# Row sums and AV of a batch in one PSUM tile, batch 0 loaded in two row ranges, and a new opening order, in attention followed by an ELU feed-forward

## The chip, the cores and the metric

The kernel runs on one core of one Trainium2 chip. The metric is the device time of the run in microseconds (us): the median of seven runs of the kernel before is 354.44 us, the lowest 353.19, the highest 355.32. A core has engines that run side by side, each through its own list of instructions in order: PE (TensorE, matrix products, which also loads weights, PEld in the profile), ACT (ScalarE), DVE (VectorE), POOL (GpSimd) and SP (SyncE). They wait for each other through semaphores. PE writes into PSUM only, which ACT and DVE read. DMA transfers are issued from POOL, SP or ACT and move on their own.

## The reference

There are 8 batches of 8 heads with 576 queries, 64 elements a head, and 16 extra keys and values ("beacons") that stand ahead of the 576 ordinary ones and that every query may see. The attention output, 4608 tokens of 512, goes through a feed-forward network with 2048 hidden elements.

```python
k_all = np.concatenate([beacon_k, k], axis=2)
v_all = np.concatenate([beacon_v, v], axis=2)
scores = scale * np.matmul(q, k_all.transpose(0, 1, 3, 2))
scores = np.where(causal, -1000000000.0, scores)
scores = scores - scores.max(-1, keepdims=True)
a = np.exp(scores)
a /= a.sum(-1, keepdims=True) + 1e-09
attn_out = np.matmul(a, v_all)
x = attn_out.transpose(0, 2, 1, 3).reshape(B * S, H * D)
h = x @ w_in
g = np.where(h > 0.0, h, np.exp(np.minimum(h, 0.0)) - 1.0)
return g @ w_out
```

## The kernel before

The kernel is written as small named steps, and two strings give the order in which they are issued. A word such as `S.1.0.2` calls step `S` with the arguments 1, 0, 2. Every engine takes its part of each step in that order. So a step that waits on one engine holds all that stands behind it on that engine.

The first string is the opening: it loads, computes attention of batches 0 to 2 and starts batch 3, and runs the feed-forward of the first 1024 tokens. The second, `BODY`, is repeated for b = 3 to 9. In it `b` is the batch and the token tile at hand, `z` is b - 1, `c` is b + 1 and `d` is b + 2. Bodies 3 to 7 hold attention and feed-forward, 8 and 9 what is left of the feed-forward. Steps whose batch or tile doesn't exist are skipped.

The steps, with their lines:

- `lk`, `load_qk` (line 119): loads q and k of a batch. Batches 0 to 2 go to staging tiles, six rows to a partition, in two or more groups of heads. Later batches are copied to a scratch tensor in DRAM (line 583) and read back by transposing DMAs from SP (`lt`, line 591), for which POOL also writes the padding and the beacon keys. There are two buffers for each kind of staging tile, and the qkd tiles of `lt` use the same ones.
- `T` (line 227): PE turns staged q and k of two heads (a pair), so that the 64 elements of a head lie across partitions. `ck` (ACT) and `cq` (DVE) copy the turned halves from PSUM to an SBUF tile, `cb` (DVE) adds the beacon keys. For batch 0, pairs 0 to 2, ACT takes k and DVE takes q; otherwise ACT copies both in one instruction.
- `S` (line 268): scores of a pair, keys across partitions, queries along the row. The causal part of the score matrix has 1664 columns for the five chunks of keys, cut into four groups of 416. `x` (line 288, ACT) is the exponential of a group for both heads, `m` (DVE) zeroes what lies above the diagonal.
- `quad` (line 307): for four heads at once, 32 output rows each, the products over all chunks of keys, with ones (row sums, step `L`) or with one half of v (steps `W`). Each chunk is one group of four matmuls that stand side by side in the array. `L` and `W` cover queries 0 to 511 only; the last 64 queries of a batch are taken by `R` (line 414) for both groups of heads, row sums and both halves at once. A tile of tag `S` has two PSUM banks: `L` and the first `W` share one, the second `W` shares one with `R`.
- `n` (ACT, lines 349 and 352): reciprocal of the row sums by a logarithm and an exponential. `M` (DVE, line 386, and line 406 for R): output times reciprocal, into the tile of feed-forward input. Batch 0 is cut at query 256 into the parts `A` and `B`, because the first two token tiles have 256 tokens.
- `F` (line 438): one PSUM bank of hidden elements. `e` and either `u` (ACT) with `k` (DVE, line 463), or `r` and `g` (both DVE), form the ELU.
- `G` (line 484): output product of the first two token tiles. `o` copies it to SBUF and `s` stores it from SP. Later tiles use `Q` (line 548), a block scheme with seven products in place of eight for the 2 x 2 blocks, with sums of weights (`wt`) and of inputs (`Z`, line 505), and `J` for its results.
- `load_v`, `load_wi`, `load_wo` (lines 126, 142, 149): loads of v and of the two weights from POOL. `warm` issues products of zeros on PE.

All loads with a conversion of type, and the scratch copies, are issued from POOL in the order in which they are written. Besides the tag `S` (two tiles of two banks), PSUM has two banks of tag `hps` and two of tag `ops`.

Of the kernel before, what the change touches and what calls it, by code (L numbers as in the profile page):

```python
# [8 lines left out]
FP32 = mybir.dt.float32  # L9
# [8 lines left out]
def kernel(  # L18
# [12 lines left out]
    P = 128  # L31
# [20 lines left out]
    Q1 = 512  # L52
    QR = S - Q1
# [71 lines left out]

    def load_v(b, js):
        if js[0] == 0:
            st.setdefault(b, [None] * 3)[2] = stage.tile([P, NKC, H, D], FP16, tag="v16", name="v16")
            nc.gpsimd.dma_start(  # L129
                out=st[b][2][0:NB, 0, :, :], in_=beacon_v[b].rearrange("h n d -> n h d"))  # L130
        for j in js:
# [3 lines left out]
                out=st[b][2][r0:r0 + n, j, :, :],  # L135
# [28 lines left out]
    for t in qks:  # L164
        nc.vector.memset(t[:, 1, SK:P * NKC], 0.0)
# [537 lines left out]
```

## Time and profile before

| What | Value |
|---|---|
| Median of seven runs | 354.44 us |
| The profiled execution, its own time | 354.55 us |
| Span of the profiled execution | 352.8 us |
| Granted TensorE clock, mean | 0.998 |
| Instructions in the trace | 10230 |
| Moved by DMA | 34.75 MB, mean 98 GB/s |
| F, 128x512 columns (L438) | 512 matmuls, 131.5 us busy |
| Row sums and AV (L316) | 1680 matmuls of batches 1 to 7 in the code, ten groups of four to a quad with R, and 192 of batch 0 |
| Exponentials of scores (L289) | 128, 106.4 us busy, mean 905 ns |
| Copies of turned q and k on ACT (L254, L258) | 3 and 9, 2.0 and 10.5 us busy |

The span runs from the first to the last instruction, and what lies around it, 1.75 us here, is in the run's time. "Busy" is the union of an engine's instructions. Instructions of one engine can overlap in the records, so the distance from one start to the next is often shorter than the duration printed. In rows of the timeline the columns are the start and the length of a stretch in us, the engine, line and operation, what is written and read with its shape, the number of instructions, and in brackets the idle time ahead of it and who ended it. In rows of the chain they are start, length, and what the time went to. "issue" is time in which the engine waited for nothing that the profile shows.

### The profile page before, as it was taken

Reading aid. Unit: us, or ns where it says so; the run is one execution under the profiler, and the core shown is the slowest. Engines: PE = TensorE matmul, PEld = TensorE weight load, DVE = VectorE, ACT = ScalarE, POOL = GpSimd, SP = SyncE. Lnnn points to the kernel's source line nnn. Section 1 sums busy time; section 2 is a strip of 40 time slices with the busy share of each in tenths; the row PEclk is TensorE's granted clock in tenths of the full one; section 3 lists DMA queues with packets and bytes.
Section 4 is the critical chain, followed back from the end, with each engine's and each line's share of the span. In section 5 each row is a group of like instructions: output and inputs, shape, how many; then the busy total and the mean of one; then the engine's idle time right before and its main releaser. Section 6 shows DMA issues by size and latency. Waiting matters only on the chain.

```text
span 352.8 us, 10230 instructions
## 1 busy us (share of the span) xinstructions
PE 339.3 (96%) x4331; PEld 210.2 (60%) x4331; DVE 232.7 (66%) x523; ACT 291.9 (83%) x495; POOL 86.8 (25%) x120
## 2 busy tenths in 40 slices
PE   8989999899999999999999989999999999999995
PEld 3557665544456566556665556556665666666684
DVE  2446874557887767766777566757676767667661
ACT  1999999699989997999799969997999587686731
POOL 8868355460074007300540022000000000000000
PEclk9999999999999999999999999999999999999999
DMA  8999999999399309990799429601100010010022
GB/s 119 165 193 180 182 205 158 144 179 169 68 159 130 46 32 90 172 168 8 95 169 157 38 65 140 123 2 33 61 32 2 32 59 32 31 61 30 33 89 91
DMA packets 127278, 34.75 MB, mean 98 GB/s; under 512 B 110848, under 2 KB 125696, under 8 KB 127232
## 3 DMA queue, kind: packets, MB, share of 16 engines
q0 software_dynamic: 93120, 18.49, 62.8%
q1 hardware_dynamic: 33536, 15.47, 20.8%
q8 instruction: 34, 0.56, 0.6%
q10 hardware_dynamic: 576, 0.13, 0.2%
q14 instruction: 12, 0.10, 0.1%
HBM read 37.22 MB, written 15.34 MB: 149 GB/s over the span
## 4 chain that ended last, share of the span: by engine, by line
PE 66%; ACT 18%; DVE 5%; POOL 4%; DMA 3%; issue 3%; DVEq 0%; POOLq 0%
PE hps L438 28%; PE ops L548 23%; ACT et L289 9%; PE lt L316 5%; PE sc L279 4%; ACT r L453 4%; ACT e L448 4%; PE ut L316 4%; DMA kst<-in_k_dram 2%; DVE gt L463 2%; DVE xT L386 2%; PE ops L484 1%; POOL v L134 1%; DMA w_in<-in_moe_w_in_dram 1%; ACT qk L258 1%
## 5 line engine op out<-in xcount | busy, mean ns | idle before, releaser
L438 PE MATMUL hps<-xT,w_in 128*128 128x512 f16 (+1 forms) x640 | 147.7, 359 | 0.1
L463 DVE SCALAR_TENSOR_TENSOR gt<-e,r 128x512 f16<-128x512 f32 x132 | 91.2, 691 | 58.3 <-ACT r L453 57.5
L289 ACT ACTIVATE et<-sc 128x832 f16<-128x832 f32 x128 | 106.4, 905 | 2.6 <-PE sc L279 2.6
L448 ACT ACTIVATE e<-hps 128x512 f32<-128x512 f32 x144 | 88.9, 618 | 21.5 <-PE hps L438 20.3
L548 PEld LDWEIGHTS <-gt 128*128 128x128 f16 x768 | 75.1, 98 | 28.9
L438 PEld LDWEIGHTS <-w_in 128*128 128x128 f16 x640 | 56.3, 98 | 46.1 <-issue 6.7
L453 ACT ACTIVATE r<-hps 128x512 f16<-128x512 f32 x132 | 82.1, 622 | 0.0
L305 DVE TENSOR_TENSOR et<-et,triu 128x256 f16<-128x256 f16 (+2 forms) x164 | 40.7, 272 | 20.8 <-ACT et L289 18.0
L548 PE MATMUL ops<-wt,gt 128*128 128x256 f16 x384 | 52.5, 273 | 0.0
L548 PE MATMUL ops<-w_out,gt 128*128 128x256 f16 x384 | 51.4, 273 | 0.0
L134 POOL DMA_DIRECT2D v<-in_v_dram x40 | 33.7, 858 | 3.3 <-DMA kst<-in_k_dram 2.6
L505 DVE TENSOR_TENSOR gt<-gt 128x1024 f16<-128x1024 f16 x48 | 32.6, 684 | 0.0
L316 PEld LDWEIGHTS <-v 128*32 128x32 f16 x1248 | 21.2, 94 | 10.5 <-issue 5.2
L279 PE MATMUL sc<-qkd 64*128 64x208 bf16 (+5 forms) x320 | 22.6, 253 | 2.3 <-DVE xT L386 1.8
L129 POOL DMA_DIRECT2D v<-in_beacon_v_dram x8 | 4.3, 542 | 67.1 <-PE ut L316 58.8
L316 PE MATMUL ut<-et,v 128*32 128x64 f16 (+6 forms) x840 | 17.1, 225 | 3.0 <-issue 2.6
L279 PEld LDWEIGHTS <-qkd 64*128 64x128 bf16 x320 | 11.3, 94 | 14.2 <-issue 10.0
L557 ACT COPY sm<-ops 128x512 f32<-128x512 f32 x24 | 15.3, 637 | 5.0 <-PE ops L548 5.0
L564 DVE TENSOR_TENSOR osb<-ops,sm 128x512 f32<-128x512 f32 x24 | 16.4, 684 | 4.3 <-issue 3.3
L386 DVE TENSOR_TENSOR xT<-lt,rl 128x448 f16<-128x448 f32 (+6 forms) x28 | 10.6, 418 | 11.2 <-ACT rl L352 11.2
L548 PE MATMUL ops<-w_out,s 128*128 128x256 f16 x128 | 17.6, 273 | 0.0
L279 PE MATMUL sc<-qk 64*128 64x208 bf16 (+11 forms) x208 | 15.4, 245 | 2.0 <-ACT et L289 1.5
(63 smaller groups left out, 280.0 us busy)
## 6 DMA issues: line engine op xcount, KB each, us to landing
out_dram<-osb SPq DMA_DIRECT2D x36, 256.0 KB, 2.2
v<-in_v_dram POOLq DMA_DIRECT2D x24, 128.0 KB, 5.1
scr<-in_q_dram POOLq DMA_DIRECT2D x5, 576.0 KB, 12.7
scr<-in_k_dram POOLq DMA_DIRECT2D x5, 576.0 KB, 15.5
w_in<-in_moe_w_in_dram POOLq DMA_DIRECT2D x16, 128.0 KB, 5.3
w_out<-in_moe_w_out_dram POOLq DMA_DIRECT2D x4, 512.0 KB, 10.9
v<-in_v_dram POOLq DMA_DIRECT2D x8, 112.0 KB, 4.4
v<-in_v_dram POOLq DMA_DIRECT2D x8, 80.0 KB, 6.3
```

Of the source, the lines that this page charges most:

```text
L134: nc.gpsimd.dma_start(out=st[b][2][r0:r0 + n, j, :, :], in_=v[b, :, ilo[j]:ilo[j] + n, :].rearrange("h s d -> s h d"),)
L279: nc.tensor.matmul(out=s[:, h, a - c0:e - c0], lhsT=t[D * h:D * (h + 1), 1, P * j:P * (j + 1)], rhs=t[D * h:D * (h + 1), 0, NB + qa + a - ...
L289: nc.scalar.activation(out=ets[b, p][:, :, GW * g:GW * (g + 1)], in_=sc[b, p, g][:, :, 0:GW], func=AFT.Exp, bias=0.0, scale=SCALE)
L305: nc.vector.tensor_tensor(out=o, in0=o, in1=triu[0:kc[j], :, t0:t0 + e - a], op=ALU.mult)
L316: nc.tensor.matmul(out=t[32 * i:32 * (i + 1), a - qa:e - qa], lhsT=ones[0:kc[j], :] if half is None else v16[0:kc[j], j, h, 32 * half:32 * ...
L386: nc.vector.tensor_tensor(out=x_tile(k)[:, cc, tok - TT * k:to - TT * k], in0=u[:, o:o + to - tok], in1=r[:, o:o + to - tok], op=ALU.mult)
L438: nc.tensor.matmul(out=h[:, n_, :], lhsT=w_in16[:, cc, P * fc:P * (fc + 1)], rhs=xt[k][:, cc, a - TT * k:e - TT * k], start=(cc == 0), sto ...
L448: nc.scalar.activation(out=eb[t, i], in_=flat(hp[t, i]), func=AFT.Exp, bias=0.0, scale=1.0)
L453: nc.scalar.activation(out=rb[t, i], in_=flat(hp[t, i]), func=AFT.Relu, bias=0.0, scale=1.0)
L463: nc.vector.scalar_tensor_tensor(out=half(t, i), in0=eb[t, i], scalar=1.0, in1=rb[t, i], op0=ALU.subtract, op1=ALU.min)
L505: nc.vector.tensor_tensor(out=o_, in0=a_, in1=b_, op=op_)
L548: nc.tensor.matmul(out=xy[t, n_][:, qd, :], lhsT=lw[:, P * qd:P * (qd + 1)], rhs=wt_[:, c, :], start=(first and qd == 0 and c == 0), stop= ...
```

## The change

It has three parts.

1. `R` is gone. A quad now covers all 576 queries in one tile of two banks: queries 0 to 111 end at the bank's border, queries 112 to 575 lie in the second bank. `L` and each `W` have such a tile of their own, so six tiles of tag `S` a batch in place of four. `n` works on 576 columns, `M` on all queries of its half. In part `B` of batch 0, both groups of heads share a tile.
2. q and k of batch 0 are loaded and turned in two ranges of rows: 0 to 255 with two rows to a partition (128 partitions), 256 to 575 with four rows (80 partitions). `T`, `ck` and `cq` take the range as an argument and copy q and k together. `w_in` is loaded in chunks of 512 hidden columns (16 DMAs as before), and loads are steps of the order.
3. The opening string is new. Most turned tiles are copied by `cq` on DVE: of the batches 1 and 2 all but one, of batch 0 six halves of eight. `lk.3.0` and the end of v of batches 2 and 3 stand late on POOL, behind the first rows of v of batch 3. In the body `W.b.0.1` and the last two `W` have moved behind the steps `S.b.3` and `S.c.0`.

```diff
+    SEGS = {0: [(0, CUT, 2), (CUT, S, 4)]}
+
+    def segs(b):
+        return SEGS.get(b, [(0, S, R)])
+
+    def seg_view(t, b, n_):
+        a, e, r = segs(b)[n_]
+        m = (e - a) // r
+        return t[0:m, OFF[b, n_]:OFF[b, n_] + H * r * D].rearrange("p (h r d) -> p h r d", h=H, r=r)
...
+    def load_qk(b, n_, h0, h1):
+        if b not in st:
+            st[b] = [stage.tile([P, H * R * D], BF16, tag=tag, name=tag) for tag in ("qst", "kst")]
+        a, e, r = segs(b)[n_]
         for src, dst in ((q, st[b][0]), (k, st[b][1])):
             nc.gpsimd.dma_start(
-                out=dst[:, h0:h1, :, :].rearrange("p h r d -> p h (r d)"),
-                in_=src[b, h0:h1, :, :].rearrange("h (p r) d -> p h (r d)", r=R),
+                out=seg_view(dst, b, n_)[:, h0:h1, :, :].rearrange("p h r d -> p h (r d)"),
+                in_=src[b, h0:h1, a:e, :].rearrange("h (p r) d -> p h (r d)", r=r),
             )
...
-    def load_wi(fa, fe):
-
+    def load_wi(c):
+        f_ = slice(512 * c, 512 * (c + 1))
         for g in range(2):
-            for i in range(4):
-                nc.gpsimd.dma_start(
-                    out=w_in16[32 * i:32 * (i + 1), 2 * g:2 * g + 2, fa:fe], in_=wi_v[i, :, g, :, fa:fe])
+            for t in range(2):
+                nc.gpsimd.dma_start(out=w_in16[:, 2 * g + t, f_], in_=wi_v[:, :, g, t, f_])
 
     def load_wo(i):
...
-    @step
-    def T(b, p):
-        if b == 0 and p < 3:
-            tps[b, p] = bank("hps", BF16, "tq"), bank("hps", BF16, "tk")
-            dsts = tps[b, p]
...
+    @step
+    def T(b, p, n_):
+        a, e, r_ = segs(b)[n_]
+        m_ = (e - a) // r_
+        if b == 0:
+            t_ = bank("hps", BF16, "tq")[:, 0:2 * (e - a)].rearrange("c (i s) -> c i s", i=2)
         else:
-            tps[b, p] = psum.tile([P, 2, 1024], BF16, tag="S", name="tp")
-            dsts = tps[b, p][:, 0, :], tps[b, p][:, 1, :]
-        for dst, src in zip(dsts, st[b]):
-            for r in range(R):
+            t_ = psum.tile([P, 2, 1024], BF16, tag="S", name="tp")[:, :, 0:e - a]
+        tps[b, p, n_] = t_
+        for i, src in enumerate(st[b]):
+            sv = seg_view(src, b, n_)
+            for r in range(r_):
                 for h in range(2):
                     nc.tensor.transpose(
-                        out=dst[D * h:D * (h + 1), PR * r:PR * (r + 1)],
-                        in_=src[:, 2 * p + h, r, :],
-                        identity=identb[0:PR, 0:PR],
+                        out=t_[D * h:D * (h + 1), i, m_ * r:m_ * (r + 1)],
+                        in_=sv[:, 2 * p + h, r, :],
+                        identity=identb[0:m_, 0:m_],
                     )
 
     @step
...
+    def drain(f, b, p, n_):
+        a, e, r = segs(b)[n_]
+        f(out=qkT[b, p][:, :, NB + a:NB + e].rearrange("c i (p r) -> c i p r", r=r),
+          in_=tps[b, p, n_].rearrange("c i (r p) -> c i p r", r=r))
+
+    @step
+    def ck(b, p, n_):
+        drain(nc.scalar.copy, b, p, n_)
+
+    @step
+    def cq(b, p, n_):
+        drain(nc.vector.tensor_copy, b, p, n_)
...
+    QA = ilo[1]
+
+    def quads(b, g, half, name):
+
+        t = psum.tile([P, 1024], FP32, tag="S", name=name)[:, 512 - QA:512 - QA + S]
+        quad(b, g, 0, QA, t[:, 0:QA], half, True)
+        quad(b, g, QA, S, t[:, QA:S], half, True)
+        return t
...
         else:
-            t = psum.tile([P, 2, 512], FP32, tag="S", name="lt")
-            quad(b, g, 0, Q1, t[:, 0, :], None, True)
-            lt[b, g], ut[b, g, 0] = t[:, 0, :], t[:, 1, :]
+            lt[b, g] = quads(b, g, None, "lt")
...
         elif g == "B":
-            g = i[0]
-            t = ut[b, "B", g, half] = bank("ops", name="ub")
-            quad(b, g, CUT, S, t[:, 0:S - CUT], half, True)
+            t = psum.tile([P, 2, 512], FP32, tag="S", name="ub")
+            for i in range(2):
+                quad(b, i, CUT, S, t[:, i, 0:S - CUT], half, True)
+            ut[b, g, half] = t[:, :, 0:S - CUT]
         else:
-            if half:
-                t = psum.tile([P, 2, 512], FP32, tag="S", name="ut")
-                ut[b, g, 1], ut[b, "R"] = t[:, 0, :], t[:, 1, :]
-            quad(b, g, 0, Q1, ut[b, g, half], half, True)
+            ut[b, g, half] = quads(b, g, half, "ut")
...
         elif g == "B":
-            g, half = i
-            scale_out(b, 2 * g + half, CUT, S, ut[b, "B", g, half][:, 0:S - CUT],
-                      rls[b, "B"][:, (S - CUT) * g:(S - CUT) * (g + 1)])
-        elif g == "R":
-            tok = b * S + Q1
-            k = tok // TT
-            for half in range(2):
+            half = i[0]
+            r_ = rls[b, g][:, 0:2 * (S - CUT)].rearrange("c (g q) -> c g q", g=2)
+            for k, a_, e_ in ((0, CUT, TT), (1, TT, S)):
                 nc.vector.tensor_tensor(
-                    out=x_tile(k)[:, half::2, tok - TT * k:tok - TT * k + QR],
-                    in0=ut[b, "R"][:, 2 * QR * (half + 1):2 * QR * (half + 2)].rearrange("c (g q) -> c g q", g=2),
-                    in1=rls[b, "R"][:, 0:2 * QR].rearrange("c (g q) -> c g q", g=2), op=ALU.mult)
+                    out=x_tile(k)[:, half::2, a_ - TT * k:e_ - TT * k], in0=ut[b, g, half][:, :, a_ - CUT:e_ - CUT],
+                    in1=r_[:, :, a_ - CUT:e_ - CUT], op=ALU.mult)
         else:
-            scale_out(b, 2 * g + i[0], 0, Q1, ut[b, g, i[0]], rls[b, g][:, 0:Q1])
-
-    @step
-    def R_(b):
-
-        t = ut[b, "R"]
-        for n, half in enumerate((None, 0, 1)):
-            for g in range(2):
-                c = QR * (2 * n + g)
-                quad(b, g, Q1, S, t[:, c:c + QR], half, c == 0)
-        lt[b, "R"] = t[:, 0:2 * QR]
-    op["R"] = R_
+            scale_out(b, 2 * g + i[0], 0, S, ut[b, g, i[0]], rls[b, g][:, 0:S])
...
     run("""
-    warm.12 bt bk cb.0.0 cb.0.1 cb.0.3 cb.0.2 warm.3 T.0.0 ck.0.0 cq.0.0 warm.4.64 S.0.0.0
-    S.0.0.1 T.0.1 x.0.0.0 cq.0.1 m.0.0.0 x.0.0.1 S.0.0.2 warm.1.64 S.0.0.3 ck.0.1 x.0.0.2 cb.1.0
-    warm.1.64 T.0.2 S.0.1.0 x.0.0.3 x.0.1.0 warm.1.64 S.0.1.1 m.0.0.2 cq.0.2 x.0.1.1 warm.2.64
...
+    lq.0.0.0.4 warm.12 ident bt bk cb.0.0 lq.0.1.0.4 warm.8 cb.0.1 cb.0.2 T.0.1.0 T.0.0.0
+    cq.0.0.0 warm.2 ck.0.1.0 S.0.1.0 x.0.1.0 cb.1.1 S.0.0.0 T.0.1.1 cq.0.1.1 T.0.0.1 warm.2
+    x.0.0.0 S.0.1.2 lq.0.0.4.8 T.0.3.0 cq.0.0.1 tri m.0.0.0 lv.0.2 S.0.1.1 T.0.2.0 x.0.1.2
+    S.0.0.2 x.0.1.1 cq.0.2.0 x.0.0.2 S.0.1.3 x.0.1.3 cb.0.3 cq.0.3.0 m.0.1.2 warm.1 lq.0.1.4.8
+    warm.1 S.0.3.0 lq.1.0.0.4 x.0.3.0 S.0.0.1 x.0.0.1 T.0.3.1 cq.0.3.1 S.0.2.0 warm.2 warm.1
+    m.0.1.3 S.0.3.2 x.0.2.0 m.0.2.0 warm.2 S.0.0.3 cb.1.0 m.0.3.0 T.0.2.1 m.0.1.0 S.0.3.3
+    T.1.0.0 cq.1.0.0 T.1.1.0 cq.1.1.0 x.0.3.2 x.0.0.3 m.0.0.3 L.0.A x.0.3.3 lv.0.0.1 W.0.A.0
+    wi.0 ck.0.2.1 m.0.3.2 S.0.2.2 n.0.A M.0.A.0 W.0.A.1 M.0.A.1 m.0.0.2 S.1.1.0 lv.0.3.4 x.0.2.2
+    S.0.3.1 S.0.2.1 F.0.1 wi.1 wi.2 x.1.1.0 x.0.3.1 x.0.2.1 u.0.1 m.0.2.2 m.0.3.3 S.0.2.3 wi.3
...
+    m.2.0.2 F.2.1 G.0.1.3 k.2.5 m.2.2.1 m.2.2.0 lk.4.0 m.2.3.0 e.2.1 u.2.1 F.2.4 k.2.10 o.0.1
+    G.1.0.0 e.2.4 u.2.4 F.2.7 S.2.1.2 e.2.7 r.2.7 x.2.1.2 S.2.3.2 x.2.3.2 g.2.7 s.0.1 F.2.6
+    G.1.1.0 u.2.6 e.2.6 F.2.11 u.2.11 S.2.3.3 wt.4.1 k.2.6 S.2.0.1 F.2.2 e.2.11 m.2.3.2 k.2.11
+    G.1.0.1 k.2.4 x.2.3.3 e.2.2 r.2.2 x.2.0.1 g.2.2 F.2.14 lv.3.0.1 e.2.14 m.2.3.1 lk.3.0 lt.3
+    G.1.1.1 u.2.14 k.2.1 m.2.3.3 S.3.0.0 S.2.2.2 x.2.2.2 Z.2.3.0 lv.2.2.3.4 G.1.0.2 F.2.12
+    x.3.0.0 e.2.12 k.2.14 S.3.0.1 x.3.0.1 r.2.12 m.2.2.2 S.3.0.2 m.3.0.1 g.2.12 x.3.0.2 F.2.15
+    e.2.15 m.2.1.2 r.2.15 G.1.1.2 m.2.1.1 S.2.2.3 m.2.0.1 m.3.0.0 S.3.0.3 x.2.2.3 m.2.2.3
...
@@ -653,13 +644,13 @@
     k.b.3 Q.z.21.28 Z.z.2.1 lv.c F.b.4 e.b.4 u.b.4 k.b.4 Q.z.28.35 J.z.1 S.b.2.0 x.b.2.0 m.b.2.0
     S.b.2.1 x.b.2.1 m.b.2.1 F.b.5 e.b.5 u.b.5 k.b.5 Q.z.35.42 Z.z.4.0 S.b.2.2 x.b.2.2 m.b.2.2
     S.b.2.3 x.b.2.3 m.b.2.3 lk.d.0 lk.d.1 F.b.6 e.b.6 u.b.6 k.b.6 Q.z.42.49 J.z.2 Z.z.4.1
-    W.b.0.1 M.b.0.1 F.b.7 e.b.7 u.b.7 k.b.7 Q.z.49.56 S.b.3.0 x.b.3.0 m.b.3.0 S.b.3.1 x.b.3.1
-    m.b.3.1 F.b.8 e.b.8 u.b.8 k.b.8 Q.z.56.63 S.b.3.2 x.b.3.2 m.b.3.2 S.b.3.3 x.b.3.3 m.b.3.3
-    F.b.9 e.b.9 u.b.9 k.b.9 Q.z.63.70 J.z.3 L.b.1 W.b.1.0 n.b.1 M.b.1.0 F.b.10 e.b.10 u.b.10
-    k.b.10 Q.z.70.77 F.b.11 e.b.11 u.b.11 k.b.11 Q.z.77.84 J.z.4 Z.b.3.0 S.c.0.0 x.c.0.0 m.c.0.0
-    S.c.0.1 x.c.0.1 m.c.0.1 F.b.12 e.b.12 u.b.12 k.b.12 Q.z.84.91 Z.b.1.0 S.c.0.2 x.c.0.2
-    m.c.0.2 S.c.0.3 x.c.0.3 m.c.0.3 F.b.13 e.b.13 u.b.13 k.b.13 Q.z.91.98 J.z.5 W.b.1.1 R.b
-    M.b.1.1 n.b.R M.b.R F.b.14 e.b.14 u.b.14 k.b.14 Q.z.98.105 F.b.15 e.b.15 u.b.15 k.b.15
+    S.b.3.0 x.b.3.0 m.b.3.0 S.b.3.1 x.b.3.1 m.b.3.1 F.b.7 e.b.7 u.b.7 k.b.7 Q.z.49.56 F.b.8
+    e.b.8 u.b.8 k.b.8 Q.z.56.63 S.b.3.2 x.b.3.2 m.b.3.2 S.b.3.3 x.b.3.3 m.b.3.3 F.b.9 e.b.9
+    u.b.9 k.b.9 Q.z.63.70 J.z.3 W.b.0.1 M.b.0.1 L.b.1 n.b.1 F.b.10 e.b.10 u.b.10 k.b.10
+    Q.z.70.77 S.c.0.0 x.c.0.0 m.c.0.0 S.c.0.1 x.c.0.1 m.c.0.1 F.b.11 e.b.11 u.b.11 k.b.11
+    Q.z.77.84 J.z.4 Z.b.3.0 W.b.1.0 M.b.1.0 W.b.1.1 M.b.1.1 F.b.12 e.b.12 u.b.12 k.b.12
+    Q.z.84.91 Z.b.1.0 F.b.13 e.b.13 u.b.13 k.b.13 Q.z.91.98 J.z.5 S.c.0.2 x.c.0.2 m.c.0.2
+    S.c.0.3 x.c.0.3 m.c.0.3 F.b.14 e.b.14 u.b.14 k.b.14 Q.z.98.105 F.b.15 e.b.15 u.b.15 k.b.15
     Q.z.105.112 J.z.6 Z.b.3.1
     """
```

## The prediction

> **What bounds the kernel now.** I read the page first, then the chain that ended last, then each engine in order of time. The page's busy rows:
>
> ```profile
> PE 339.3 (96%) x4331; PEld 210.2 (60%) x4331; DVE 232.7 (66%) x523; ACT 291.9 (83%) x495; POOL 86.8 (25%) x120
> PE 66%; ACT 18%; DVE 5%; POOL 4%; DMA 3%; issue 3%; DVEq 0%; POOLq 0%
> ```
>
> PE carries two thirds of the chain, ACT a fifth. The shares differ by stage. The opening list ends at about 99.9 us (first block of F.3.0); five bodies with attention follow, 36.7 us apart (W and row-sum stretches at 106.6, 143.6, 180.3); from about 285 us only the feed-forward loop is left at 1.63 us a step, untouched by the change. The bodies, PE in order of time:
>
> ```profile
> 155.95 0.35 PE L279 MATMUL sc<-qkd 64*128 64x160 bf16 x4 [0.37 <-DVE xT L386]
> ...
> 160.17 0.76 PE L316 MATMUL lt<-et,ones 128*32 128x512 f16 x20
> 160.77 0.74 PE L316 MATMUL lt<-et,v 128*32 128x512 f16 x20
> 161.45 1.04 PE L438 MATMUL hps<-xT,w_in 128*128 128x512 f16 x4
> ...
> 169.20 0.76 PE L316 MATMUL ut<-et,v 128*32 128x512 f16 x20
> 169.81 0.49 PE L316 MATMUL ut<-et,ones 128*32 128x64 f16 x40
> 170.10 0.85 PE L316 MATMUL ut<-et,v 128*32 128x64 f16 x80
> 170.89 1.04 PE L438 MATMUL hps<-xT,w_in 128*128 128x512 f16 x4
> ```
>
> Durations overlap, so I use start to start. Two quads of 20 take 161.45-160.17 = 1.28 us; the remainder R (120 matmuls of 64 columns) takes 170.89-169.81 = 1.08 us, 9.0 ns each, 36 ns for four that share the array. PE is the bound here, with one hole: S.3.1 waits for the buffer that M.b.0.1 (line 386) frees. The chain shows the others:
>
> ```profile
> 22.43 3.89 DMA w_in<-in_moe_w_in_dram
> 26.33 0.34 PE sc L279 x2
> 26.67 1.85 PE hps L438 x16
> ...
> 64.48 1.14 issue
> ...
> 207.65 1.44 issue
> ```
>
> The first F starts at 26.67, as soon as the eighth w_in load lands; and twice PE stands still with no releaser, both inside an R or at its end.
>
> **Opening, engine sums.** From 26.6 to 99.9 us (73.3 us) PE has 16 narrow F at 0.93, 16 wide F at 0.865, 16 G at 0.86, 35 S at 0.23, 6 T at 0.55, and row sums and AV of 3.05 (rest of batch 0) + 4.9 + 5.15 (batches 1 and 2, without the hole): 28.7+13.8+8.0+3.3+13.1 = 66.9 us, 91%. ACT has 36 exps at 0.755 (start to start; the row mean of 905 ns overlaps), 32 e and 20 u at 0.48, 6 turn copies at 1.01 and 7.2 of logs: 65.5 us. Both are nearly full. Before 26.6, ACT runs without gap from 9.78: 16 exps, the batch 0 turns, one log pair.
>
> **The change, part by part.**
>
> *Row sums and AV (quads).* A quad had groups of 512, 400, 272, 144, 16 columns plus five of 64 in R: ten groups of four. It now has 112, 464, 464, 336, 208, 80: six groups, the same 1664 columns, 672 matmuls fewer over 42 quads. Price by the row: 0.64 us for the five large groups less 36 ns for the issue-limited 16-column one is 0.604 us for 1328 columns, 0.455 ns a column; the new quad is 1584 x 0.455 + 36 = 0.757 us, or 0.69 us at the 512-column row's best rate (an F of 2048 columns in 0.86). Before, the four stretches of a body are 1.48+0.69+1.28+1.69 = 5.14 us, of which 0.1 waits for exps; after, 6 x 0.757 + 0.1 = 4.64 (bound 4.25). I take 0.5 to 0.9 saved, 0.6: five bodies, 3.0 us. The Trainium skill speaks against this: "TensorEngine Tiling (Array Packing)", Instruction Overhead, has a matmul of 1 column cost the same as one of 60, so groups of 64 would pay nothing extra: the old quad is (1328+60+320)/2.4 = 712 ns, the new 693, and a body gains 0.11 us, five 0.6. The row has 36 ns, not 27, for 64 columns, so I go by the row.
>
> *The fetch holes.* The page's DMA queues show 34 instruction packets of 0.56 MB, 65 bytes for each of PE's 2 x 4331 instructions. "Runtime: NRT & Kernel Launch", Instruction fetch mechanics, calls the refill mostly hidden; by it nothing is gained. The trace has 1.14 and 1.44 us in the two places where PE consumes some 220 instructions in a microsecond (2 x 120 in 1.08 us). R's 64-column burst is gone (48 instructions in 0.75 us), so I take both: 1.1 in the opening, 1.4 in the bodies; bounds 0 and 2.6.
>
> *Body order.* W.b.0.1/M.b.0.1 move behind S.3.3, so S.3.1 no longer waits (0.37 visible; 155.23 to 156.24 against 0.46 for a free pair is 0.55 lost). The next user of that buffer, S.c.0.0, comes F+Q+L = 2.35 us later. On DVE M queues behind k.9, which waits for u.9 on an ACT that runs about a microsecond late after three S steps: M could end near 2.4 us, so 0.15 may remain. 0.4 x 5 = 2.0 us; bounds 0 and 2.75. Six S-tag tiles a batch instead of four make n.b.1 a new wait of S.c.0.1; it has about the same slack. ACT loses 0.586 us of R's logs and gains 0.23 of wider ones; DVE loses two of ten M: both hidden under PE.
>
> *Turns.* Most copies of turned q/k go from ACT (9 x 1.0, 3 x 0.52) to DVE: ACT gets about 8 us lighter, DVE about 11 heavier (7 at 1.35 and 6 halves at 0.75, less 3 at 0.68): 69 of 100 us before, 80 after. It isn't the longest queue, but m and k stand behind these copies, so this gain pays only where ACT holds PE.
>
> *First F.* PE's eight warm matmuls after the beacon turn (was three) put the first turn near 8.9 and the first exp near 10.4 (was 9.78). But ACT then has 12 exps, one half copy and the log pair before F.0.1's input: 10.4 + 9.1 + 0.5 + 1.4 = 21.4, M twice 22.7, S.0.2.1 behind x.1.1.0 about 23.2. w_in comes in column chunks; up to its first chunk 2.7 MB are due, and the trace moved 2.6 MB by 18 us, 4.3 by 27: landed near 20. The second chunk, for F.0.3, lands near 24 where F.0.3 stands at 24.8. T.1.3 (5.3 MB, about 33 us) and w_out (5.8 MB, about 36) stand at 34 and 39 on PE. So F begins near 23.6, 3.0 us earlier, if 256-byte pieces of q/k load as fast. After it PE has 28.7+13.8, 36 S 8.3, T 3.3, all of batch 0's second range 3.7 and 12 quads 9.1: 66.9 us, as before. I keep the old idle: gain 3.0; bounds -4 and 8 (PE at 98%). POOL issues as many q/k and w_in loads as before at 0.53 to 0.76 each, and its queue is paced by landings, so I charge it nothing; if the cover goes, F.0.3 waits for what w_in is late.
>
> *Scratch chain.* On POOL lk.3.0 now stands behind lv.3's beacon rows, which wait for W.1.0.0. PE has 31 us of work up to that, so near 57 us; the scratch copy is issued near 61 and lands 8.5 to 12.7 later. On SP the transposes stand behind s.0.0/s.0.1, near 74. They were:
>
> ```profile
> 63.24 9.38 SPq L591 DMA_TRANSPOSE qkd<-scr  x4
> 72.72 20.95 SPq L497 DMA_DIRECT2D out_dram<-osb  x4
> ```
>
> Two issues at 1.75 to 2.35 and a landing of 5.8 give 82 to 84; S.3.0.0, 86.88 before, is due at 83 on PE. I charge 1.1 us; bounds 0 and 4.
>
> **Sum.** 3.0 + 2.0 + 1.4 (bodies) + 3.0 + 1.1 - 1.1 (opening) = 9.4 us. The profiled execution spans 352.8 us and took 354.55, 1.75 around it; its span becomes 343.4, the run 345.1. The median shown is 354.44, so 345.0.
>
> **Rivals.** (a) The opening gains nothing: DVE, with 80 us, holds m and k late, or data does; bodies still give 6.4 and the fetch hole 1.1: 347 to 349. For it: two engines are 90% full and DVE joins them. Against: in the opening's list of waits PE waits for ACT and for fetches, not for DVE. (b) ACT was what held PE: with 8 us less, PE runs at 98% and the opening gives 8: 338 to 341. (c) The column rule holds and bodies give only the wait: 3 to 4 us in all, 350. (d) Slower: S.3.0.0 stands in order on PE, and everything behind it with it. If transposes land after 83 + 9.4, about 92.5 us, the gain is gone; were the scratch to take the trace's longest 19.4 us and the transposes 12.5 as at 139 us, they land near 95, and the time is about 357. Against it: the queue has drained by then.
>
> **How the numbers follow.** Forecast 0.46; (a) 0.19, (b) 0.12, (c) 0.10, (d) 0.13. A difference under 0.3%, 1.06 us, can't be told from none. (a), (b) and all but 0.02 of (c), which may give nothing, are faster: faster 0.85, same 0.02, slower 0.13. The forecast's own range is 342 to 348; with (b) and (c) whole and part of (d) it is 338.5 to 352.5.
>
> **What would show it.** 1008 row-sum and AV matmuls for batches 1 to 7 (1680 before), none of 64 columns; W+L of a body near 4.6 us; body spacing near 35.6; no issue hole over 1 us at L316; no PE wait on M; first F near 23.6; F.3.0 near 97; S.3.0.0 waiting at most 4 us. Wrong if the spacing stays above 36.3, if PE waits for q, k, w_in or qkd in the opening by over 3 us, or DVE becomes the releaser of S.

## The result and the profile after

The changed kernel takes 351.81 us (median of 15 runs, 348.59 to 353.83) against 354.16 us for the kernel before (36 runs, 353.19 to 356.37): a ratio of 0.9933 with a 95% interval of 0.9917 to 0.9949. It is faster by 2.35 us, where 9.4 us were forecast. The direction held; the time lies outside the forecast's own range of 342 to 348 us and just inside the wide one of 338.5 to 352.5. The ratios here and below leave out one run of this kernel (353.83 us) and one of e9 (845.53 us) as slow. The profiled execution spans 350.3 us, against 352.8 us before.

The busy row and the shares of the chain, from the page after:

```profile
PE 335.4 (96%) x3649; PEld 204.3 (58%) x3651; DVE 242.3 (69%) x514; ACT 281.1 (80%) x473; POOL 91.5 (26%) x120
PE 81%; ACT 5%; DMA 5%; DVE 4%; POOL 3%; issue 1%; DVEq 0%; ACTq 0%; POOLq 0%
```

PE has 682 matmuls fewer and 81% of the chain instead of 66%; ACT's share fell from 18% to 5%, which fits its lighter share of the turns. But DMA rose from 3% to 5%, and there the forecast broke. One body of the changed kernel, PE in order of time:

```profile
182.65 0.90 PE L322 MATMUL lt<-et,ones 128*32 128x112 f16 x24
183.39 0.90 PE L322 MATMUL ut<-et,v 128*32 128x112 f16 x24
184.22 1.04 PE L432 MATMUL hps<-xT,w_in 128*128 128x512 f16 x4
...
203.46 1.61 PE L322 MATMUL ut<-et,v 128*32 128x112 f16 x48
204.99 1.04 PE L432 MATMUL hps<-xT,w_in 128*128 128x512 f16 x4
```

Read start to start, two quads take 184.22-182.65 = 1.57 us, the last two 204.99-203.46 = 1.53; with 1.54 for the two between, row sums and AV take 4.64 us of a body (5.14 before, 4.64 forecast). L.b.0 starts at 147.09, 182.65 and 218.20: 35.56 us apart, forecast 35.6. No wait of PE between 106 and 290 us remains in the list of waits, where before it held 1.8 us for xT and 1.4 us of issue. From the start of F.3.0 to the end it is 350.3-105.25 = 245.05 us, against 352.8-99.85 = 252.95 before: 7.9 us gained where 6.4 were forecast.

So the whole miss lies ahead of F.3.0. It starts at 105.25 us, 5.4 us later than before; 3.0 us earlier was forecast. And -7.9+5.4 is the -2.5 us between the two spans. Two stretches of the chain show where (start, duration, what):

```profile
12.93 9.86 DMA w_in<-in_moe_w_in_dram
...
23.07 0.66 POOL w_in L159
23.73 6.63 DMA w_in<-in_moe_w_in_dram
30.36 0.05 issue
30.41 1.25 PE hps L432 x5
...
55.58 2.84 DVE qk L259
...
73.95 2.33 DVE r L464
```

The first F starts at 24.46, close to the forecast of 23.6. But F.0.3 has only its first three of eight matmuls done when it stands still for w_in, and the rest runs at 30.41, when the load that POOL began to issue at 23.07 has landed. POOL had stood still for 4.35 us between 15.65 and 23.07, each time until an earlier load landed. Later two small DVE operations, a copy of 16 columns and a minimum over 512, are on the chain with 2.8 and 2.3 us. PE's list of waits for the opening puts numbers on both:

```profile
PE hps L432 <- DMA w_in<-in_moe_w_in_dram: 3.8, 3, 1.8
PE sc L285 <- ACT et L295: 1.6, 4, 0.7
PE hps L432 <- DVE gt L469: 1.0, 1, 1.0
PE ut L322 <- DVE qk L263: 1.0, 1, 1.0
```

There is a third loss, which no list of waits names. The table by stretches has, behind the busy times of PE, PEld, DVE, ACT and POOL, the granted TensorE clock, the DMA share and GB/s; first three rows of the changed kernel, then the same stretches of the kernel before:

```profile
27.00:30.00 3.00, 0.83 (x3) 0.29 (x3) 1.06 (x3) 0.39 (x1) 2.05 (x4) 1.00 1.18 135
30.00:33.00 3.00, 2.59 (x33) 1.55 (x37) 0.19 (x1) 1.09 (x2) 2.06 (x3) 0.50 1.12 116
33.00:36.00 3.00, 3.00 (x75) 2.06 (x68) 0.51 (x1) 1.13 (x2) 1.26 (x2) 0.93 1.32 157
```

```profile
27.00:30.00 3.00, 3.00 (x44) 2.15 (x43) 1.58 (x4) 2.73 (x5) 3.00 (x6) 1.00 1.05 176
30.00:33.00 3.00, 3.00 (x60) 2.20 (x58) 2.38 (x6) 2.67 (x5) 2.59 (x4) 1.00 1.22 175
33.00:36.00 3.00, 3.00 (x64) 2.05 (x62) 2.47 (x8) 3.00 (x6) 1.44 (x2) 1.00 1.26 208
```

In the stretch in which PE starts again after its pause, its clock is 0.50. So W.0.B.1, the first of the next two rows, takes 33.54-31.59 = 1.95 us, against 28.94-27.85 = 1.09 us for the same 40 matmuls at full clock in e4, which the rows after it show (PE in order of time):

```profile
31.59 2.12 PE L322 MATMUL ub<-et,v 128*32 128x320 f16 x40
33.54 1.24 PE L322 MATMUL lt<-et,ones 128*32 128x320 f16 x40
```

```profile
27.85 1.25 PE L328 MATMUL ub<-et,v 128*32 128x320 f16 x40
28.94 1.25 PE L328 MATMUL lt<-et,ones 128*32 128x320 f16 x40
```

That is 0.86 us there and some 0.6 us on the five matmuls of F.0.3 (1.18 us against eight in 0.98). And in all these stretches the DMA moves 116 to 157 GB/s where it moved 175 to 208.

### The profile page after: what moved, and what is told of

Same layout as the page of the kernel before. It is cut to its first block, busy times and chain, and to the rows that moved or that the text cites. A ratio compares the mean times of both kernels' runs of the same rounds, so it can differ in the third digit from the quotient of the medians.

```text
span 350.3 us, 8837 instructions
## 1 busy us (share of the span) xinstructions
PE 335.4 (96%) x3649; PEld 204.3 (58%) x3651; DVE 242.3 (69%) x514; ACT 281.1 (80%) x473; POOL 91.5 (26%) x120
## 4 chain that ended last, share of the span: by engine, by line
PE 81%; ACT 5%; DMA 5%; DVE 4%; POOL 3%; issue 1%; DVEq 0%; ACTq 0%; POOLq 0%
PE hps L432 34%; PE ops L542 28%; PE ut L322 6%; PE sc L285 6%; DMA w_in<-in_moe_w_in_dram 5%; PE lt L322 3%; PE ops L478 3%; ACT et L295 2%; ACT e L442 1%; POOL kst L134 1%; DVE r L464 1%; DVE qk L259 1%; POOL qst L134 1%; ACT r L447 1%; POOL v L147 1%
## 5 line engine op out<-in xcount | busy, mean ns | idle before, releaser
L432 PE MATMUL hps<-xT,w_in 128*128 128x512 f16 (+1 forms) x640 | 149.5, 360 | 5.1 <-DMA w_in<-in_moe_w_in_dram 3.8
L447 ACT ACTIVATE r<-hps 128x512 f16<-128x512 f32 x133 | 83.2, 627 | 6.8 <-PE hps L432 4.3
L147 POOL DMA_DIRECT2D v<-in_v_dram x40 | 35.3, 972 | 5.0 <-DMA qst<-in_q_dram 1.5
L322 PE MATMUL ut<-et,v 128*32 128x464 f16 (+4 forms) x672 | 23.6, 283 | 1.0 <-DVE qk L263 1.0
L396 DVE TENSOR_TENSOR xT<-ut,rl 128x448 f16<-128x448 f32 (+7 forms) x56 | 22.3, 453 | 2.8 <-ACT rl L364 2.3
L322 PEld LDWEIGHTS <-v 128*32 128x32 f16 (+1 forms) x800 | 17.4, 98 | 11.7 <-issue 5.0
L285 PE MATMUL sc<-qkd 64*128 64x208 bf16 (+5 forms) x320 | 21.6, 252 | 0.0
L551 ACT COPY sm<-ops 128x512 f32<-128x512 f32 x24 | 16.2, 673 | 5.0 <-PE ops L542 5.0
L285 PE MATMUL sc<-qk 64*128 64x208 bf16 (+10 forms) x208 | 15.4, 246 | 2.8 <-ACT et L295 2.5
```

Source lines behind the costliest of these rows:

```text
L147: nc.gpsimd.dma_start(out=vt[b][r0:r0 + n, j, :, :], in_=v[b, :, ilo[j]:ilo[j] + n, :].rearrange("h s d -> s h d"),)
L285: nc.tensor.matmul(out=s[:, h, a - c0:e - c0], lhsT=t[D * h:D * (h + 1), 1, P * j:P * (j + 1)], rhs=t[D * h:D * (h + 1), 0, NB + qa + a - ...
L322: nc.tensor.matmul(out=t[32 * i:32 * (i + 1), a - qa:e - qa], lhsT=ones[0:kc[j], :] if half is None else v16[0:kc[j], j, h, 32 * half:32 * ...
L396: nc.vector.tensor_tensor(out=x_tile(k)[:, cc, tok - TT * k:to - TT * k], in0=u[:, o:o + to - tok], in1=r[:, o:o + to - tok], op=ALU.mult)
L432: nc.tensor.matmul(out=h[:, n_, :], lhsT=w_in16[:, cc, P * fc:P * (fc + 1)], rhs=xt[k][:, cc, a - TT * k:e - TT * k], start=(cc == 0), sto ...
L447: nc.scalar.activation(out=rb[t, i], in_=flat(hp[t, i]), func=AFT.Relu, bias=0.0, scale=1.0)
```

## The experiments

Differences between kernels are read from the ratios to the kernel before, which each set of runs carries. As a mark for the opening I use the start of L.3.0, the first row sums of the first body: it stands behind the same steps of the body in every kernel. It is at 106.62 us before and 111.53 us after. A profile shows one run; where its time is not typical for its kernel, that is said.

### The bodies alone (e1)

The kernel before with `quads` in L and W, M over all 576 columns, R, n.R and M.R dropped from the lists, and the changed kernel's body list:

```diff
-            t = psum.tile([P, 2, 512], FP32, tag="S", name="lt")
-            quad(b, g, 0, Q1, t[:, 0, :], None, True)
-            lt[b, g], ut[b, g, 0] = t[:, 0, :], t[:, 1, :]
+            lt[b, g] = quads(b, g, None, "lt")
...
-            scale_out(b, 2 * g + i[0], 0, Q1, ut[b, g, i[0]], rls[b, g][:, 0:Q1])
+            scale_out(b, 2 * g + i[0], 0, S, ut[b, g, i[0]], rls[b, g][:, 0:S])
```

> The kernel before with the new quads and the new body order; its opening order, its loads and its turns are the old ones (R is only dropped from the list). My theory: the loss lies in the new opening alone. Then the bodies are 35.6 us apart as in the changed kernel (36.7 before), the first block of F.3.0 starts at 98 to 99.5 us (99.85 before; the fetch hole of 1.1 us at the second batch's R is gone), and the time is 346 to 348 us, below the changed kernel's 351.8. Rival: the new opening is needed for the bodies' gain (ACT or DVE would be late without it), and the time stays at 350 to 352.

Measured: 347.78 us (347.21 to 348.95), ratio 0.9812 [0.9791, 0.9834]. The new body on the old opening is 4 us faster than the changed kernel and gives most of what the whole change was to give. Its bodies are 35.55 us apart (L.4.0 to L.5.0: 144.04 to 179.59), so they don't need the new opening. One expectation failed: the opening was to be earlier by the fetch hole, and L.3.0 stands at 108.49, 1.9 us later than before. The profiled run is the slowest of its four, 1.7 us above the fastest, and PE waits in it for a load. From PE's list of waits ahead of 106 us (engine, line, what it waited for, us, times, longest):

```profile
PE ut L316 <- ACT et L289: 1.7, 2, 0.8
PE sc L279 <- ACT et L289: 1.5, 5, 0.7
PE tp L237 <- DMA kst<-in_k_dram: 0.9, 1, 0.9
```

### The two halves of the body's gain (e7 and e8)

e7 moves two words in the body list of the kernel before. e8 is e1 with the old order of the body, R's words left out.

```diff
-    W.b.0.1 M.b.0.1 F.b.7 e.b.7
+    F.b.7 e.b.7
...
-    Q.z.63.70 J.z.3 L.b.1
+    Q.z.63.70 J.z.3 W.b.0.1 M.b.0.1 L.b.1
```

> The kernel before with W.b.0.1 and M.b.0.1 moved behind S.b.3.3 in the body and nothing else (the remainder R stays). By the prediction's price (0.4 us a body) the bodies come 36.3 us apart instead of 36.7, the wait of S.3.1 on M is gone, and the time falls by 2.0 us to 352.6. Rival: the wait goes on to the next user of the buffer, the spacing stays at 36.6 to 36.8 and the time at 354.2 to 355.

> The kernel before with the row sums and AV of all 576 queries in one two-bank tile (no remainder R), in the old body order and the old opening. By the prediction's price (0.6 us a body, five bodies, and the fetch holes of 1.14 and 1.44 us) the time falls by 5.5 us to 349.1, with no issue hole over 1 us at the row sums and AV. By the column rule (0.11 us a body, holes kept) it falls by 0.6 us to 354.0. If the holes stay but the bodies gain, 351.6.

e7: 351.32 us, ratio 0.9918 [0.9902, 0.9933], bodies 36.08 us apart (142.85 to 178.93). e8: 350.86 us, 1.8 above what was expected, ratio 0.9901 [0.9888, 0.9914], bodies 36.27 us apart (143.08 to 179.35). Against 36.70 before, the moved W is worth 0.62 us a body and the quads 0.43; together 1.05 of the 1.14 that the changed kernel has. So the total was right and the split was not: forecast were 0.4 and 0.6. Nothing of the wait stayed behind in e7; the 0.15 us that I had left for it was not there. In e8 the wait is still there, as it should be (PE in order of time):

```profile
155.64 0.35 PE L279 MATMUL sc<-qkd 64*128 64x160 bf16 x4 [0.30 <-DVE xT L390]
```

The fetch holes: in e8's chain no piece of issue is longer than 0.5 us. In e7's chain, which keeps R, they stand where they were:

```profile
64.49 1.01 issue
...
205.68 1.24 issue
```

In the kernel before, the body with the hole is 38.33 us long (180.27 to 218.60) instead of 36.70; in e8 all are within 0.03 us of each other. So the bodies' hole is 1.6 us really gained over the profile before. It is not always that long: in the profile of e5 below, which keeps R, PE stands 0.3 us there, and that body is 37.15 us. That the holes go with R is shown; that they are fetches is inferred. The opening's hole is not gained: L.3.0 of e8 is at 106.83, no earlier than before, because PE now comes to the row sums earlier and waits 1.7 us for ACT's exps there, as in the list shown for e1.

### The form of the w_in loads (e2 and e5)

e2 is the changed kernel with the old form, all 1024 columns of a pair of chunks at the place of the first of them. e5 makes the reverse edit in the kernel before.

```diff
-    def load_wi(c):
-        f_ = slice(512 * c, 512 * (c + 1))
-        for g in range(2):
-            for t in range(2):
-                nc.gpsimd.dma_start(out=w_in16[:, 2 * g + t, f_], in_=wi_v[:, :, g, t, f_])
+    def load_wi(c):
+        if c % 2:
+            return
+        f_ = slice(512 * c, 512 * (c + 2))
+        for g in range(2):
+            for i in range(4):
+                nc.gpsimd.dma_start(
+                    out=w_in16[32 * i:32 * (i + 1), 2 * g:2 * g + 2, f_], in_=wi_v[i, :, g, :, f_])
```

> The changed kernel with the old form of the w_in loads: eight DMAs of 32 partitions for each 1024 columns, at the places of the first and the third chunk, instead of four DMAs of 128 partitions for each 512. Theory A, the new form is slow by itself (8.1 us to land against 5.3, 384 near-empty packets each): the landing falls back to 5 to 6 us, F.0.3 no longer waits 3.8 us for w_in, the first block of F.3.0 starts near 101.5 instead of 105.25, and the time is 347.5 to 349. Theory B, the DMAs ahead of it (256-byte pieces of q and k) are what is late: the landing stays at 7 us or more, PE still waits 3 us or more for w_in, and the time stays at 351 to 352.5.

> The kernel before with the new form of the w_in loads alone (128 partitions by 512 columns, sixteen DMAs, the first 1024 columns first, at the old places); all else is old. Theory A, the form is slow by itself: the median landing rises from 5.3 us to over 7, the DMA moves under 150 GB/s in the 18 to 27 us stretch (187 before), the first F, which waits for the first 1024 columns, starts at 28.5 to 31 instead of 26.67, and the time rises by 2 to 4.5 us to 356.5 to 359. Theory B, the form is harmless and the 256-byte pieces of q and k are what delayed w_in: the first F stays within 0.7 us of 26.67 and the time within 1 us of the kernel before.

The two edits are not quite each other's reverse. e5 changes the form alone. e2 also moves the second chunk forward, ahead of the last values of batch 0, so its gain is that of form and place together.

e2: 349.19 us, ratio 0.9847 [0.983, 0.9864], 0.0086 below the changed kernel, 3.0 us. The median landing is 5.6 us (8.1), L.3.0 stands at 108.72 (111.53), and PE's wait for w_in is 2.0 us in one piece (PE in order of time):

```profile
24.66 0.39 PE L435 MATMUL hps<-xT,w_in 128*128 128x256 f16 x2
27.02 1.01 PE L435 MATMUL hps<-xT,w_in 128*128 128x256 f16 x6 [1.97 <-DMA w_in<-in_moe_w_in_dram]
```

e5: 357.61 us, ratio 1.0076 [1.0053, 1.0099]. The form alone makes the kernel before 2.7 us slower. Its landing is 7.3 us (5.2 to 6.2 in e1, e7, e8 and the kernel before, which have the same opening with the old form), and the DMA moves 157 GB/s from 18 to 27 us (174 to 200 in those). Where the 2.7 us go its profile doesn't tell: the profiled run took 354.50 us, the fastest of eight (the others 356.67 to 358.28). Its first F starts at 26.67 as before, not at 28.5 to 31 as Theory A had it. L.3.0 stands at 107.69, 1.1 us later than before, and the short hole named above makes up for that. The packet rows of e5 and of before, each for the whole span:

```profile
q0 software_dynamic: 100288, 18.51, 64.2%
```

```profile
q0 software_dynamic: 93120, 18.49, 63.0%
```

The form adds 7168 packets and no bytes to speak of: 1024 because a row is cut at 512 columns instead of 1024, and 6144 more, 384 for each of its sixteen DMAs of 128 rows. By the times, the form costs what Theory A says in both directions. But it isn't all: with the old form the changed kernel still waits 2.0 us, and from 18 to 27 us the DMA moves 154 GB/s, up from 135 but far from 187.

### The held DVE operations (e3)

In cb and r of the changed kernel (`one` is a tile of ones, 128x512 f16):

```diff
-        nc.vector.tensor_copy(out=qkT[b, p][:, 1, 0:NB], in_=bkT[:, p, NB * b:NB * (b + 1)])
+        nc.vector.tensor_tensor(
+            out=qkT[b, p][:, 1, 0:NB], in0=bkT[:, p, NB * b:NB * (b + 1)], in1=zero[:, 0:NB], op=ALU.add)
...
-        nc.vector.tensor_scalar(
-            out=rb[t, i], in0=eb[t, i], scalar1=1.0, scalar2=1.0, op0=ALU.min, op1=ALU.subtract)
+        nc.vector.scalar_tensor_tensor(
+            out=rb[t, i], in0=eb[t, i], scalar=1.0, in1=one, op0=ALU.min, op1=ALU.subtract)
```

> The changed kernel with two DVE operations given a second source: the copy of the beacon columns adds a tile of zeros, and e's min and subtract takes its one from a tile of ones. Theory: an operation with a single source in SBUF waits for something that GpSimd holds while it issues a scratch copy (2.66 to 2.92 us at 55.5, 2.32 us at 73.95), one with two sources doesn't (masks ran in 0.28 us under the scratch copies of the kernel before). Then no DVE row of that stretch exceeds 0.8 us, PE's waits of 0.96 us at 60.1 and 1.00 us at 77.1 go, and the time falls by 1 to 2 us to 350 to 351. Rival: DVE stood still for another reason (its semaphores, or the memory), and both rows stay above 2 us and the time at 351.5 to 352.5.

DVE and POOL in the changed kernel, in order of time (an operation behind the held one in the queue shows the time that it stood there):

```profile
55.50 2.92 DVE L259 COPY qk<-bkT 128x16 bf16<-128x16 bf16 x1
55.57 2.85 DVE L311 TENSOR_TENSOR et<-et,triu 128x256 f16<-128x256 f16 x1
55.63 2.79 POOL L573 DMA_DIRECT2D scr<-in_q_dram  x1
...
58.59 1.45 DVE L263 COPY qk<-tp 128x1152 bf16<-128x1152 bf16 x1
...
73.26 2.76 POOL L573 DMA_DIRECT2D scr<-in_k_dram  x1
...
73.95 2.32 DVE L464 TENSOR_SCALAR r<-e 128x512 f16<-128x512 f32 x1 [0.73 <-ACT e L442]
```

And in e3, where the order is the same and only the copy and the minimum have a second source:

```profile
54.30 2.77 POOL L576 DMA_DIRECT2D scr<-in_q_dram  x1
54.88 0.28 DVE L314 TENSOR_TENSOR et<-et,triu 128x256 f16<-128x256 f16 x1
55.08 0.16 DVE L261 TENSOR_TENSOR qk<-bkT,zero 128x16 bf16<-128x16 bf16 x1
55.16 1.35 DVE L266 COPY qk<-tp 128x1152 bf16<-128x1152 bf16 x1
...
72.87 2.76 POOL L576 DMA_DIRECT2D scr<-in_k_dram  x1
...
73.83 0.69 DVE L467 SCALAR_TENSOR_TENSOR r<-e,one 128x512 f16<-128x512 f32 x1 [0.73 <-ACT e L445]
```

Under the same 2.77 us of issue the 16-column copy takes 0.16 us instead of 2.92, and the minimum 0.69 instead of 2.32. PE's waits of 1.0 us for qk and for gt are gone from its list, and the time is 350.44 us, ratio 0.9883 [0.9868, 0.9898]: 0.0050, or 1.8 us, below the changed kernel. So these operations with one source in SBUF are held while GpSimd issues a scratch copy; with two sources they are not, nor is a copy whose source is in PSUM (55.16). The hold has limits. It is long with the scratch copies only: under the shorter issues of loads, a single copy of 16 columns takes 0.15 to 0.58 us in the kernel before, e1 and e5, and a minimum 0.41 to 0.86 us. And it doesn't cover the first moments: in e2 a minimum that starts 0.37 us into such an issue takes 0.42 us (50.29). The Trainium skill has the rule in "SBUF — State Buffer", section "SBUF: two separate sides": DVE and GpSimd share a port pair under an exclusive lock, for DVE operations in a mode that uses both pairs or with two sources in SBUF (these only against a GpSimd operation that reads SBUF); whichever starts first has the lock for its whole instruction, and the other waits. The box in that section warns of a DVE operation that keeps GpSimd from writing descriptors; these rows show the other direction. That the held operations were in such a mode no run here shows.

### Both, and the order of the loads (e4 and e6)

e4 has the edits of e2 and e3. e6 adds one edit of the opening list:

```diff
-    warm.1 S.0.3.0 lq.1.0.0.4 x.0.3.0
+    warm.1 S.0.3.0 x.0.3.0
...
-    T.1.0.0 cq.1.0.0 T.1.1.0 cq.1.1.0 x.0.3.2
+    x.0.3.2
...
-    m.0.0.2 S.1.1.0 lv.0.3.4 x.0.2.2
+    m.0.0.2 lq.1.0.0.4 lv.0.3.4 x.0.2.2
...
-    F.0.1 wi.1 wi.2 x.1.1.0 x.0.3.1
+    F.0.1 wi.1 wi.2 x.0.3.1
...
-    F.0.3 u.0.3 m.0.2.3
+    F.0.3 u.0.3 T.1.0.0 cq.1.0.0 T.1.1.0 cq.1.1.0 S.1.1.0 x.1.1.0 m.0.2.3
```

> Both of the last two edits in the changed kernel. If the w_in wait and the held DVE operations are two separate losses, their gains add: the first block of F.3.0 starts near 99.5 and the time is 345.5 to 347.5. If one hides the other (PE 3.8 us earlier only waits longer for DVE or ACT), it is no better than the better of the two, 348 to 350.

> The changed kernel with the old form of the w_in loads, the two-source operations of e3, and one more edit of the order: the first half of batch 1's q and k (0.58 MB) is issued behind the first 1024 columns of w_in instead of ahead of the values of batch 0, and its two turns and S.1.1.0 stand behind F.0.3. If what is left of the loss is bytes that stand ahead of w_in, PE waits less than 1 us for w_in, the granted clock stays at 1.00 in the stretch from 24 to 40 us, and the time is 344.5 to 346, with a spread under 2 us (345.39 was the best of e4, whose runs reach 350). Rival: the turns of batch 1 are now late, PE or ACT waits for kst or qk instead, and the time is 347 to 350.

e4: 348.5 us, 345.39 to 350.01, ratio 0.9817 [0.9762, 0.9872]. The gains of e2 and e3 don't add reliably: the four runs are 4.6 us apart, and the interval takes in that of e2. In the profiled one (349.59) the wait for w_in has only moved on to the next chunk (PE in order of time):

```profile
25.84 0.81 PE L438 MATMUL hps<-xT,w_in 128*128 128x256 f16 x6 [0.71 <-DMA w_in<-in_moe_w_in_dram]
...
34.36 1.37 PE L438 MATMUL hps<-xT,w_in 128*128 128x256 f16 x6 [2.58 <-DMA w_in<-in_moe_w_in_dram]
```

e6: 349.23 us, ratio 0.9832 [0.9804, 0.9861], so the rival was right. There is no wait for w_in any more, but the turns of batch 1 are late in its place, and the clock is 0.50 from 30 to 36 us all the same. PE in order of time:

```profile
27.25 0.45 PE L255 MATMUL tp<-identb,kst 96*64 96x96 bf16 x12 [1.18 <-DMA kst<-in_k_dram]
...
30.41 0.53 PE L291 MATMUL sc<-qk 64*128 64x416 bf16 x2 [2.21 <-DVE qk L269]
30.88 2.27 PE L328 MATMUL ub<-et,v 128*32 128x320 f16 x40
```

It looks as if the bytes that come by about 30 us are too few for what the new opening asks by then, so that reordering them only chooses what is late. No run with fewer bytes tests that.

### Work put into the pause (e9, e10 and e11)

e9 is the changed kernel with these words of the opening list in another order:

```diff
-    x.0.2.3 e.0.1 F.0.3 u.0.3 m.0.2.3 W.0.B.1 k.0.1 L.0.B e.0.3 F.0.0 k.0.3 S.1.1.3 F.0.5 n.0.B M.0.B.1
+    x.0.2.3 e.0.1 m.0.2.3 W.0.B.1 k.0.1 L.0.B n.0.B M.0.B.1 F.0.3 u.0.3 e.0.3 F.0.0 k.0.3 S.1.1.3 F.0.5
```

e10 is e9 with the edits of e3. e11 is e10 with w_in in the old form, in chunks of 512 columns (32 DMAs).

> The changed kernel with one edit of its order: W.0.B.1, L.0.B, n.0.B and M.0.B.1 stand ahead of F.0.3 instead of behind it, so PE has 2.3 us of work that needs no w_in while the second chunk lands. w_in arrives no earlier. If PE's pause of 3.8 us and the half clock after it (0.50 in the stretch from 30 to 33 us, the row sums and AV of batch 0 at twice their time) are what the late w_in costs, the wait falls to 1 to 2 us, the clock stays at 0.9 to 1.0, and the time falls by 2.5 to 4 us to 348 to 349.3. Rival: PE only waits later by as much, and the time stays within 1 us of 351.8.

> The order of e9 and the two-source operations of e3 together. If both losses are separate, the time is 1.4 us below e9, 346.6 to 348, close to the 347.8 of e1, whose opening is the old one; with both removed it is what the prediction promised but for w_in's last microsecond or two. Rival: with PE earlier, DVE and ACT are late instead and the time stays at 348.5 to 350.

> As e10, with w_in in the old form but in chunks of 512 columns: eight DMAs of 32 partitions by two row groups by 512 columns, 32 in all instead of 16. If the form of the new loads is what makes them late, the landing falls to 5 to 6 us, the wait of F.0.3 goes altogether and the time is 345 to 346.5. Rival: POOL issues 32 DMAs at 0.53 us, 17 us instead of 10.7, which delays what it issues behind them (the second half of batch 1's q and k, w_out), and the time is 347 to 350.

e9: 353.84 us, ratio 0.996 [0.993, 0.999]: no faster than the changed kernel (0.9933), where a gain was expected. The pause did shrink, to 2.1 us in four pieces, and the clock stays at 1.00 up to 60 us. But the later work now meets the scratch copies at a worse moment, and the held copy stops DVE for both of them (DVE and POOL in order of time; the first row is a copy that still ran freely, 0.11 us after the first scratch copy's issue began at 54.24):

```profile
54.35 0.16 DVE L259 COPY qk<-bkT 128x16 bf16<-128x16 bf16 x1
...
54.62 4.11 DVE L259 COPY qk<-bkT 128x16 bf16<-128x16 bf16 x1
...
55.87 4.47 DVE L263 COPY qk<-tp 128x1152 bf16<-128x1152 bf16 x1
55.96 2.78 POOL L573 DMA_DIRECT2D scr<-in_q_dram  x1
```

PE then waits 1.4 and 1.0 us for DVE, and its clock falls to 0.50 from 62 to 64 us. With two sources, e10 takes 349.44 us, ratio 0.983 [0.9783, 0.9876]: the same two-source edit that gave 1.8 us in e3 gives 0.013 or 4.6 us here. The cost of a held operation is a matter of where it falls. Against e3 the filled pause gives 0.0053, 1.9 us, less than the 2.5 to 4 expected, and the two intervals overlap: PE still waits 2.2 us for w_in, and its clock falls to 0.50 a little later, from 36 to 39 us. e11: 352.41 us, ratio 0.9939 [0.9903, 0.9975]. Each load, now of half the size, lands in 3.9 us, but 32 of them cost GpSimd 16.9 us instead of 10.8, and PE waits 4.6 us for w_in. The rival, too many issues, fits, though it allowed for no more than 350 us.

## Why the prediction was wrong

That the kernel is faster at all is the bodies' doing: they gained more than forecast and hid an opening that lost what it was to gain.

1. *Quads:* the mechanism was right. By the trace of the bodies row sums and AV fell by 0.50 us, by e8's spacing a body fell by 0.43. The forecast's own sum, 5.14 less 4.64, is 0.50 too; the 0.6 was taken above it. The column rule (the Trainium skill's "TensorEngine Tiling (Array Packing)", Instruction Overhead) gave an estimate of 0.11. The row of 36 ns for four 64-column matmuls was the better guide.
2. *Body order:* right, and undersized: 0.62 us a body in e7, forecast 0.4.
3. *Fetch holes:* both are gone with R (e8) and stay with it in e7; in e5 the second shrinks to 0.3 us. The bodies' one was worth 1.6 us, forecast 1.4. The opening's 1.1 us was not gained even with the old opening: PE waits for ACT instead.
4. *First F and what follows:* this step failed. I had the first chunk landed near 20 us and the second near 24, from the volume that the kernel before had moved by then, "if 256-byte pieces of q/k load as fast"; and I charged POOL's queue nothing. The load that F.0.3 waits for last was issued only by 23.73, behind POOL's waits for landings, and landed 6.6 us later; five matmuls of F.0.3 run at 30.4 instead of 24.8. PE's wait of 3.8 us for w_in is over the 3 us that I had named as a sign of being wrong. The rate was not the old one: 135 GB/s from 18 to 27 us instead of 187. In time, the new w_in form costs 2.7 us in the old opening (e5), and form and place together 3.0 in the new one (e2). Of the rate, e2 gives back only 19 of the 52 GB/s; what takes the rest is not shown, and the 256-byte pieces stay a suspect.
5. *Not in the sum at all:* the half clock after a pause of PE (1.4 us in the profile shown), and DVE operations held by GpSimd's issues (1.8 us by e3). I had read the DVE column as 80 of 100 us busy and no releaser; what counted was which kind of DVE operation lies under a scratch copy. In the kernel before there was none.
6. *Scratch chain:* no cost in this run. S.3.0.0 starts at 92.52 without a wait, but PE itself was late; whether the chain would have held a PE that was on time is not shown.
7. *The rivals:* (a), the opening gains nothing "or data does", had the right cause but stopped at zero; the opening lost 5.4 us. Its time of 347 to 349 is what e1 has. (b) is out: ACT is busy 10.8 us less (281.1 against 291.9), and the opening is no shorter. (c) is out by e8's 0.43 us a body, and what (d) feared did not come (point 6).

Added up as waits of the one profile, the 8.4 us between +5.4 and -3.0 are 3.8 (w_in), about 1.4 (clock) and 2.0 (held DVE); some 1.2 us are not assigned. The experiments bear the sizes out only in part: e2 and e3, which take up the first and the last, gain 3.0 and 1.8, and e4, which has both, can't be told from e2.

What stays open: whether the new order would give its 3 us if the data were in time. Nothing here shows it. The best run of e4, 345.39 us with a span of 343.7, puts L.3.0 at about 105.0 (an estimate: the 238.7 us from L.3.0 to the end in e1, taken from that span), 1.6 us ahead of the kernel before. Not tried were the 256-byte pieces by themselves, nor the new order with fewer bytes ahead of w_in. Why the form of 128 rows is slow is not shown either: the extra packets are a sign of it, not a proof.

The lowest median of all these kernels is that of e1, the old opening with the new bodies: 347.78 us, below both kernels compared here. e4 and e10 can't be told from it.

## What to carry to other kernels

Split a change by stage and time the stages apart: here one half was worth 6.7 us (e1) and the other took more than 4 of them back, and the sum looked like a small success. When an order is pulled earlier, recount the bytes due by each point at the rate that the new loads reach, and remember that a change of a load's shape is a change of that rate. A pause of a few microseconds on PE costs more than itself; and a small single-source DVE operation under GpSimd's issue of a scratch copy can take 2 to 4 us, which a second source avoided here.

## What the runs showed of the hardware that was not expected

- The granted clock fell to 0.50 after PE had been busy only 0.83 of 3 us, and 40 matmuls took 1.95 us start to start instead of 1.09. The Trainium skill's "TensorE: Matmul & The Clock Gate", What's actually happening, says that an idle window of about 3.4 us halves the clock. The stretch from 25.8 to 30.4 us is longer than that but not idle, since three matmuls ran in it. In e9 pauses of at most 0.6 us, broken by work, left the clock at 1.00; in e10 it fell after pauses of 0.9 and 1.2 us with matmuls between.
- A DVE copy of 16 columns took 2.92 us under a scratch copy's issue of 2.79 us, and 0.16 us with a second source. Under the issues of loads such copies took at most 0.58 us with one source.
- A load of 128 rows by 512 columns whose source rows come from four blocks makes 384 packets more than its 128 rows account for, almost without bytes. The median load lands in 7.3 to 8.1 us, against 5.2 to 6.2 for the old form of the same size.
- The spread between runs differs from kernel to kernel: e8's four runs lie within 0.5 us, e5's eight within 3.8, the changed kernel's fifteen within 5.2. Where in a run it arises, no profile here shows.
